# A second temporary for the spectrum products, one tile for what lay in two, and joint instructions in an S4/GEGLU kernel

## The chip, the cores and the metric

The kernel runs on one core of a Trainium2 chip. The metric is the device time of one execution in microseconds (us). The engines are PE (TensorE), PEld (its weight loads), DVE (VectorE), ACT (ScalarE), POOL (GpSimd) and SP (SyncE, which here issues nearly all DMA transfers).

## The reference

The kernel mixes two branches over the same input of 2048 positions and 640 channels. Branch a is an S4 convolution: a kernel K of length 2048 is built for each channel from 128 complex modes, and u is convolved with it, in the reference by FFT. Branch b is a GEGLU feed-forward layer with 1728 hidden columns.

```python
x = A_u
g = sigmoid((x * gate_w).sum(-1, keepdims=True))
P = exp((dt * A)[:, :, None] * l[None, None, :])
K = einsum("dn,dnl,dn->dl", Cc, P, dt * Bc).real
...
y = irfft(rfft(u, 2 * L) * rfft(K, 2 * L))[:L] + u * Dskip
b = (gelu(x @ w_gate) * (x @ w_up)) @ w_down
out = g * y + (1 - g) * b
```

## The kernel before

**Tiling.** Positions are handled in two halves of 1024 (th 0 and 1) for the feed-forward layer, channels in two halves of 320 (h 0 and 1, W2 = 320) for the convolution. The hidden columns are 14 blocks of 128, the last half full.

**Stages.** Gate and up projections: steps `g{ft}.{th}` and `u{ft}.{th}`, each 10 matmuls of 128x512 (`gu`, L381); `h.{th}` is block 13, whose 64 gate and 64 up columns share one result. The weights come in pairs of blocks, step `lw{n}`, into two slots (L277, L278). Results leave PSUM by `eg`/`eu` steps, copies on ACT (L386) or DVE (L388). What doesn't stay in SBUF goes to DRAM: the copy writes one of three slots named `ring`, an `sg`/`su` step sends the slot off (L408), and `rg`/`rl` steps bring it back later (L694 for the up part), where `hm` multiplies (L695). A ring slot is given to each use in turn when the steps are defined, so in the order of definition, not of emission.

Fold of the input: `uf{c}.{r}` (L372) writes sums and differences into `pm0`, `us{c}` sends them to DRAM, `lu{h}{c}` brings them back.

The table of K: for each h, exponentials (`xa`, `xb`), then chunks of phases and sines. A chunk of kind b takes `fb` (`phase_b`, L481, one DVE instruction for each of up to three blocks), `qb` (L469, the cosine's phase), `sb` (`sin_b`, L490: two sines of 128x960) and the products `pb`, `pc` (L495, L508); kind a takes `fa` (L474), `qa`, `sa` (L484, one sine of 128x1920), `pa` (L499). The sines write the buffer T. Then `ct{h}.{j}` contracts the tables on PE (L520, L521), `ek{h}.{j}` unloads (two copies of 128x504, one for each bank), `ks` adds the skip term (L587), `kd.{h}` sends the raw table Kraw to DRAM in four transfers that each read every fourth partition (`regroup_out`, L536), and `kt.{h}` brings it back in another arrangement.

Spectra: `U...` (L706) and `K...` (L719) on PE, evicted by ACT. Products on DVE: `m{h}{c}{i}{part}` multiplies a spectrum of u with one of K. The first two of a chunk write P and X directly (L761); the later ones write the one temporary t (L764), and `s{h}{c}{i}{part}` adds t to P or X (L765). `y{h}{c}0/1` (L767, L768) closes the chunk. Then the inverse `I` (L779), the down projection `D` (L794), the mix `Z` (L801, L802), the scaled eviction `o` and the store `st`.

**What sets the order.** The string ORDER lists all steps by name, and `manual_schedule` emits them in exactly that order; each engine and SP's queue of transfers work off theirs in the order of emission. A suffix `/A` or `/D` picks ACT or DVE, `/0` to `/3` a PSUM bank. The waits between engines are derived from which earlier instructions read or wrote the same tile.

**Memory.** `early` (29,696 bytes in each partition), `work` and `tail` (19,200) are tiles in which many buffers are laid over each other (`lay`). In `early` lie the fold's buffers (uf, ur and pm0, bytes 0 to 10239), later Kraw0 from byte 16128, later spectra. In `tail` lie T, al, th and other inputs of the table, later Kraw1 and IM, later Ub0, Kb0 and pmb.

Of the kernel before, what the change touches and what calls it, by code (L numbers as in the profile page):

```python
# [40 lines left out]
lp0 lpk ldt idx one tdt/0 tabE dt oa.0 sk leu2 lp5 lw0 lp3 t0/1 al xb23.0 xa4.0 xb6.0 xa10.0 al2 xa5.0 xa17.0 lp4 x0.0  # L41
lp2 t4/2 t2/3 xb4.0 xa19.0 c2 xb9.0 xb14.0 x1.0 t5/0 x4.0 x3.0 lp1 t3/1 c3 x2.0 v0 v3 ur0 ob.0 xa9.0 xb17.0 xb2.0
xb1.0 xb13.0 xa1.0 xa3.0 v1 v5 v2 t1/3 ul0 th v4 xb12.0 v6 v7 xb5.0 xa8.0 xb8.0 fb0.0 fb1.0 qb0.0 g1.0/1 eg1.0/D v8
uf0.1 v11 uf0.0 u1.0/2 xb21.0 xb11.0 v9 xa16.0 xb15.0 v10 xa11.0 xb3.0 xb27.0 xa14.0 eu1.0/D g0.0/0 u0.0/3 eu0.0/A v12
v13 v14 mag xb31.0 v15 xa7.0 xb7.0 xb29.0 xb25.0 xb19.0 xb10.0 xa15.0 v16 tabT sb0.0 x4.1 lw1 qb1.0 eg0.0/D g3.0/1
eg3.0/D ma3.0 ma0.0 v17 ma1.0 ul1 us0 ma4.0 ma6.0 u3.0/2 u2.0/3 g2.0/0 lw2 su0.0 leu3 lw3 su1.0 eu3.0/A eg2.0/A sb1.0
u4.0/1 eu2.0/A ur1 uf1.0 v18 uf1.1 ur2 fb2.0 pc0.0 qb2.0 pb0.0 pb1.0 pc1.0 fb3.0 qb3.0 us1 su2.0 sb2.0 eu4.0/A su4.0
lgw su3.0 lsk pb2.0 pc2.0 at g4.0/2 eg4.0/A sb3.0 ph45 fb4.0 qb4.0 g5.0/0 u7.0/3 eg5.0/A u5.0/1 eu5.0/A fb5.0 pc3.0
qb5.0 pb3.0 sb4.0 lw4 sb5.0 u6.0/2 eu6.0/A g7.0/0 g6.0/1 eu7.0/A eg7.0/A ma2.0 fa0.0 pc4.0 qa0.0 pb4.0 eg6.0/A sa0.0
g8.0/2 eg8.0/A u8.0/3 g9.0/0 x0.1 x2.1 lw5 x3.1 ul2 su7.0 su6.0 x1.1 lw6 su5.0 fa1.0 pb5.0 qa1.0 fa2.0 qa2.0 pa0.0  # L50
sa1.0 eg9.0/A fa3.0 sa2.0 pa1.0 u10.0/1 eu10.0/A qa3.0 sa3.0 pa2.0 u9.0/2 eu9.0/A fa4.0 qa4.0 pa3.0 fa5.0 sa4.0 fa6.0
qa5.0 pa4.0 qa6.0 eu8.0/A g11.0/0 u12.0/1 u11.0/2 eg11.0/A sa5.0 ma5.0 fil.0 pa5.0 g10.0/3 su8.0 su9.0 lu00 lw7 leu0
h.0/0 sa6.0 pa6.0 eu12.0/A eg10.0/D ct0.4/1 ek0.4/D eu11.0/A ct0.0/2 ct0.6/3 ek0.6/D uf2.0 uf2.1 ct0.3/1 ek0.0/A
eg13.0/A ct0.2/2 ct0.1/3 ek0.1/D ek0.3/A su10.0 su12.0 su11.0 ct0.5/1 ek0.2/D ek0.5/D ur3 oa.1 ob.1 u12.1/3 tabE2
xb8.1 fil.1 eu12.1/D ks.0 xa7.1 xb29.1 xb27.1 xb9.1 xa1.1 xb13.1 ma0.1 xa8.1 xb3.1 xa9.1 xa10.1 xb4.1 xa14.1 xb19.1
# [10 lines left out]
K000/3 eK001/D pa5.1 eK000/A K011 K012 K013 K010 pa6.1 eK012/A eK013/A eK010/D eK011/D tabG m0000 ct1.4/1 ct1.2/2
ek1.2/D ek1.4/A ge1.0 sg7.1 lw13 ct1.3/3 ek1.3/A ct1.1/0 ct1.5/1 ek1.5/A ct1.6/2 ek1.1/D rl1.0 su7.1 gl2 hm0.0 ct1.0/0
lu01 rl3.0 rl2.0 hm1.0 rl4.0 rg2.1 lkb1 rg13.1 lkb0 g9.1/3 ek1.0/A ek1.6/A dg9 m0001 gl3 y001 y000 U012/1 U011/0
eU011/D U010/2 eU012/D U013/3 ge3.0 eU010/A eU013/A ks.1 m0100 g11.1/0 ge5.0 ge9.0 dg11 kd.1 u11.1/1 g8.1/2 m0111
hm2.0 m0110 hm4.0 s0100 rl5.0 hm5.0 du11 hm3.0 dg8 m0101 g10.1/3 u8.1/0 gf/2 gf1 du8 s0101 dg10 ge7.0 ge11.0 u10.1/1  # L70
# [10 lines left out]
K110 K102/1 eK110/A K113 D020/2 eK102/A eK121/A eK113/A pm2/A s0320 m0321 s0321 m0330 s0330 m0331 s0331 y030 y031
m1001 m1000 K133/0 K112 eK112/A Z020 K122/3 eK122/A y101 m1100 eK133/A o020/A pm3/A D021/1 Z021 st010 st011 lwd1 lu12
lu13 st020 o021/A U132/3 U123/0 eU123/A I031/2 I030/1 m1110 y100 m1111 s1100 m1101 K130/0 eI031/A eK130/A eU132/A
eI030/A D030/2 U120/0 U122/3 eU120/A eU122/A I100/1 Z030 eI100/A U121/0 I101/3 D031/1 Z031 o030/A m1210 lwe1 eI101/A
eU121/A U131/2 eU131/A U130/3 eU130/A o031/A D100/0 K123/2 K120/3 eK120/A Z100 eK123/A s1101 y110 y111 m1220 m1211
s1220 I110/1 eI110/A m1221 s1221 m1200 s1200 m1201 st021 st030 st031 K132/3 eK132/A I111/2 U133/1 eU133/A o100/A
eI111/A m1310 D101/3 K131/1 eK131/A s1201 m1320 y120 y121 s1320 m1311 m1321 s1321 m1330 s1330 m1331 s1331 m1300 s1300
m1301 s1301 y130 y131 Z101 D110/0 D111/2 Z111 st100 o101/A st101 o111/A Z110 I120/1 I121/3 eI121/A eI120/A D120/2
o110/A st110 st111 Z120 o120/A st120 D121/3 Z121 o121/D D130/1 I130/0 eI130/A I131/2 Z130 o1301/A o1300/A eI131/D
D131/3 Z131 o1310/D st121 st1300 st1301 st1310 o1311/D st1311  # L90
# [54 lines left out]
def kernel(  # L145
# [253 lines left out]
    turn_no = [0]  # L399

    def ring():
        turn_no[0] += 1
        return at["ring"][:, turn_no[0] % at["ring"].shape[1]]

    def spill(which, name, eng_step, src, dst, rows):
        r = ring()
        step(eng_step, lambda eng="A", r=r: copy(eng, halves(r[0:rows]), PS[bank[name]][src]))
        step(f"s{which}", lambda r=r: S.dma_start(out=dst, in_=r[0:rows]))  # L408
# [469 lines left out]
```

## Time and profile before

| | us |
|---|---|
| runs | 288.59, 290.98, 292.38 |
| median of the three | 290.98 |
| span of the profiled execution | 287.8 |
| ACT busy | 221.0 (77%) |
| POOL busy | 16.0 (6%) |
| gate and up matmuls, L381, x526 | 120.9 |
| sums of products, L765, x24 | 35.7 |
| down matmuls, L794, two groups x224 | 31.7 and 31.4 |

The time that the profiled execution itself took is not listed apart from these runs; the page gives its span alone. In the rows below, `out<-in` names the tiles, `x` the number of instructions, and a bracket the idle time of the engine before them with what ended it. Rows of several instructions give the stretch from the first start to the last end. SPq is SP's queue of transfers; its times are those of issuing, not of landing. The windows view lists the busy time of PE, PEld, DVE, ACT and POOL, the granted TensorE clock as a share, the DMA share and GB/s.

### The profile page before, as it was taken

To read this page: it belongs to the slowest core of one execution; us is meant where nothing else is said; L and a number is where in the kernel's file an instruction comes from. 1 tells how busy PE (TensorE), PEld (TensorE's weight loads), DVE (VectorE), ACT (ScalarE), POOL (GpSimd) and SP (SyncE) were. 2 spreads that over 40 slices of the span, in tenths; PEclk is the share of its full clock that TensorE was granted. 3 is DMA by queue.
4 is the path that set the end of the run, shared out by engine and by line. 5 is a ranking of instruction groups with operands and counts; after the bars stand their busy time and mean duration, and the time that the engine had idled before them with its cause. 6 is when DMAs were issued, how large, how long until landed. Compare 5 with 4: busy or idle time off the path is not lost.

```text
span 287.8 us, 4927 instructions
## 1 busy us (share of the span) xinstructions
PE 264.4 (92%) x1869; PEld 159.4 (55%) x1883; DVE 261.7 (91%) x339; ACT 221.0 (77%) x321; POOL 16.0 (6%) x23
## 2 busy tenths in 40 slices
...
GB/s 207 207 224 193 132 298 178 211 236 118 182 224 202 200 308 227 226 272 259 234 76 223 206 193 294 235 80 179 109 284 73 2 23 23 25 23 2 68 23 46
DMA packets 64300, 46.94 MB, mean 163 GB/s; under 512 B 23403, under 2 KB 54166, under 8 KB 64278
## 3 DMA queue, kind: packets, MB, share of 16 engines
...
q0 software_dynamic: 384, 1.31, 1.7%
q10 hardware_dynamic: 576, 0.43, 0.5%
...
## 4 chain that ended last, share of the span: by engine, by line
DVE 47%; PE 30%; DMA 7%; issue 6%; ACT 4%; SPq 4%; POOL 0%; DVEq 0%; ACTq 0%
PE ps L381 25%; DVE work L764 11%; DVE work L765 11%; DVE work L761 8%; DMA work<-Ud 2%; DVE H L695 2%; SPq L285 2%; DVE work L388 2%; DVE work L767 2%; DMA xT<-in_A_u_dram 2%; DMA early<-in_A_u_dram,back 2%; DVE work L695 2%; DVE work L768 2%; ACT tail L490 1%; PE ps L794 1%
## 5 line engine op out<-in xcount | busy, mean ns | idle before, releaser
L381 PE MATMUL ps<-xT,Wr 128*128 128x512 bf16 x526 | 120.9, 386 | 6.5 <-ACT work L386 2.3
L381 PEld LDWEIGHTS <-Wr 128*128 128x128 bf16 x540 | 53.4, 99 | 70.9 <-issue 8.8
L386 ACT CAST work<-ps 128x640 bf16<-128x640 f32 (+1 forms) x59 | 47.8, 839 | 24.8 <-PE ps L779 15.7
L765 DVE TENSOR_TENSOR work<-work 128x2560 bf16<-128x2560 bf16 x24 | 35.7, 1487 | 0.5
L794 PE MATMUL ps<-xT,work 128*128 128x320 bf16 x224 | 31.7, 299 | 0.0
L794 PE MATMUL ps<-xT,H 128*128 128x320 bf16 x224 | 31.4, 299 | 0.0
L794 PEld LDWEIGHTS <-H 128*128 128x128 bf16 x224 | 21.9, 98 | 8.5
L794 PEld LDWEIGHTS <-work 128*128 128x128 bf16 x224 | 21.9, 98 | 8.5
L484 ACT ACTIVATE tail<-work 128x1920 bf16<-128x1920 int16 x14 | 25.2, 1816 | 0.5 <-DVE work L469 0.4
L508 DVE TENSOR_TENSOR work<-tail,work 128x1920 bf16<-128x1920 bf16 (+1 forms) x22 | 23.8, 1093 | 0.5 <-ACT tail L490 0.5
L392 ACT ACTIVATE Wr<-ps,gs 128x320 bf16<-128x320 f32 x28 | 13.2, 526 | 13.1 <-issue 9.5
L779 PE MATMUL ps<-work,tail 128*128 128x320 bf16 x128 | 19.7, 299 | 3.0 <-DVE work L767 3.0
L490 ACT ACTIVATE tail<-work 128x960 bf16<-128x960 int16 (+1 forms) x24 | 20.7, 927 | 0.0
L474 DVE SCALAR_TENSOR_TENSOR work<-tail 128x320 int32<-128x320 f32 x42 | 17.9, 483 | 0.5 <-ACT tail L484 0.5
L779 PEld LDWEIGHTS <-tail 128*128 128x128 bf16 x128 | 12.3, 98 | 9.0 <-DVE work L767 4.0
L706 PEld LDWEIGHTS <-early 128*128 128x128 bf16 x128 | 12.4, 98 | 7.0 <-issue 1.4
L469 DVE TENSOR_SCALAR work<-work 128x960 int32<-128x960 int16 (+1 forms) x26 | 16.1, 627 | 0.1
L499 DVE TENSOR_TENSOR work<-tail,work 128x1920 bf16<-128x1920 bf16 x14 | 15.9, 1150 | 0.0
L719 PE MATMUL ps<-KTt,early 128*128 128x320 bf16 x80 | 15.5, 313 | 0.5 <-ACT early L392 0.3
L365 POOL DMA_INDIRECT early<-in_A_u_dram,back x8 | 11.0, 1371 | 67.3 <-DVE early L372 57.0
L392 ACT ACTIVATE work<-ps 128x640 bf16<-128x640 f32 x15 | 10.4, 714 | 5.3 <-PE ps L719 5.2
L462 ACT ACTIVATE work<-tail 128x320 bf16<-128x320 f32 x30 | 12.5, 456 | 2.0 <-DVE tail L324 2.0
(120 smaller groups left out, 411.8 us busy)
## 6 DMA issues: line engine op xcount, KB each, us to landing
...
```

The source lines that it names most:

```text
L381: P.matmul(t[:, x, :], lhsT=Wr[:, slot, kt, cols:cols + 128], rhs=xT[:, th, kt, 512 * x:512 * x + 512], start=(kt == 0), stop=(kt == 4))
L386: A.copy(out=out, in_=in_)
L392: act(out=out, in_=in_, func=ACT.Copy, scale=scale)
L474: stt(out=t[:, 0, x], in0=at["th"][:, d], scalar=float(A_OF[3 * c + x] + MID), in1=at["ph45"][:, d], op0=ALU.mult, op1=ALU.add)
L484: act(out=T, in_=low16(t)[:, :, :, ::2], func=ACT.Sin, scale=SIN_SCALE)
L490: act(out=o[:, r], in_=i[:, r], func=ACT.Sin, scale=SIN_SCALE)
L508: tt(out=B2[:, :, :, cols].rearrange("p r g x -> p g r x"), in0=Tv if hf == 0 else Tv[:, :, ::-1], in1=e, op=ALU.mult)
L761: step(f"m{h}{c}{i}{part}", lambda dst=dst, ux=ux, kx=kx: tt(out=fl(dst), in0=ux, in1=kx, op=ALU.mult))
L764: step(f"m{h}{c}{i}{part}", lambda ux=ux, kx=kx: tt(out=fl(t), in0=ux, in1=kx, op=ALU.mult))
L765: step(f"s{h}{c}{i}{part}", lambda dst=dst, op=op: tt(out=fl(dst), in0=fl(dst), in1=fl(t), op=op))
L779: P.matmul(t[:, r, 0:W2], lhsT=IM[:, e, m, r], rhs=Y[:, r, m], start=(m == 0), stop=(m == 3))
L794: P.matmul(t[:, x, 0:W2], lhsT=H[c // 2][:, ft, tk:tk + 128], rhs=at[f"Wd{h}"][:, ft], start=(ft == 0), stop=False)
```

## The change

1. **Second temporary.** The products of part 1 write t1 instead of t, and ORDER moves the second product of a pair ahead of the first sum (m, m, s, s where it was m, s, m, s).
2. **One tile.** `early` and `tail` become one tile `side` of 49,664 bytes, in which t1 has room. T lies at byte 30464, Kraw0 stays at 16128, Kraw1 moves to 36224.
3. **Raw table of K.** Its layout goes from [4, NA, NG] to [NA, 4, NG], so that `ek` copies both banks with one instruction.
4. **One sine.** `sin_b` is one instruction of 128x1920; for it `phase_b` writes its result in blocks of four int32.
5. **Half tile.** `h.{th}` is copied once with 128 rows. For th 0 the up half is sent to DRAM from H0; for th 1 both halves from one ring slot, and `sg13.1` moves forward in SP's queue to stand directly ahead of `su13.1`.
6. **Ring slots** are taken from a list of free ones at emission and given back with the last use.
7. **Permutations.** flip and flipn are scaled by one instruction: four instead of six for each chunk.

SP's queue around `kd.0`, before: the spill of `u12.1`, the weights `lw8`, `kd.0`, then `sg12.1`, `su13.0`, `sg0.1` and `lw9`. The bracket names the semaphores waited for: DMAHW for a transfer, DVE, PE or Activation for a count on that engine.

```order
L278 DMA Wr<-in_B_w_up_dram 128x5x256 [waits DMAHW3_49]
L536 DMA Kd_70<-early 672x1x80 [waits DMAHW0_49,DMAHW4_49,DVE_49,Activation_49]
L536 DMA Kd_70<-early 672x1x80 [waits DMAHW5_49]
L536 DMA Kd_70<-early 672x1x80 [waits DMAHW6_49]
L536 DMA Kd_70<-early 672x1x80 [waits DMAHW7_49]
L408 DMA Gd<-work 128x1024 [waits DVE_49]
L408 DMA Ud_67<-work 64x1024 [waits DMAHW1_49]
L408 DMA Gd<-work 128x1024 [waits DMAHW2_49,DVE_49]
L277 DMA Wr<-in_B_w_gate_dram 128x5x256 [waits DMAHW3_49,PE_49]
L278 DMA Wr<-in_B_w_up_dram 128x5x256 [waits DMAHW4_49]
```

The same place of SP's queue after the change:

```order
L275 DMA Wr<-in_B_w_up_dram 128x5x256 [waits DMAHW3_49]
L538 DMA Kd_70<-side 672x1x80 [waits DMAHW4_49,DMAHW0_49,Activation_49]
L538 DMA Kd_70<-side 672x1x80 [waits DMAHW5_49]
L538 DMA Kd_70<-side 672x1x80 [waits DMAHW6_49]
L538 DMA Kd_70<-side 672x1x80 [waits DMAHW7_49]
L411 DMA Gd<-work 128x1024 [waits DVE_49]
L425 DMA Ud_67<-H_78 64x1024 [waits DMAHW1_49]
L411 DMA Gd<-work 128x1024 [waits DMAHW2_49,DVE_49]
L274 DMA Wr<-in_B_w_gate_dram 128x5x256 [waits DMAHW3_49,PE_49]
L275 DMA Wr<-in_B_w_up_dram 128x5x256 [waits DMAHW4_49]
```

The transfers stand in the same sequence; what moved is what the first of `kd.0` waits for. Before, its counts belong to `uf3.1` on DVE and `ek0.3` on ACT; now there is one count on ACT, and it is that of `sb0.1`, the first sine of half 1.

ACT behind the last exponential of half 1, before: the table load, the two sines of `sb0.1`, the eviction `eg1.1`, the two sines of `sb1.1`.

```order
L561 ACT_TABLE_LOAD
L490 ACTIVATE tail<-work 128x3x80x4 [waits DVE_49,Activation_49]
L490 ACTIVATE tail<-work 128x3x80x4 [waits DVE_49]
L386 CAST work<-ps_65 128x1024 [waits DMAHW5_49,DMAHW0_49,DMAHW6_49,DVE_49,PE_49]
L490 ACTIVATE tail<-work 128x3x80x4 [waits Activation_49]
```

And after:

```order
L563 ACT_TABLE_LOAD
L493 ACTIVATE side<-work 128x1920 [waits DVE_49,Activation_49]
L383 CAST work<-ps_65 128x1024 [waits DMAHW0_49,DMAHW5_49,DVE_49,PE_49]
L493 ACTIVATE side<-work 128x1920 [waits DMAHW5_49,DMAHW6_49,DMAHW4_49,DMAHW7_49,DVE_49,Activation_49]
L383 CAST work<-ps_66 128x1024 [waits DMAHW5_49,DMAHW1_49,DMAHW6_49,DVE_49,PE_49]
```

Each pair of sines is one, the sines write `side`, and the second chunk's sine (`sb1.1`) waits for the four transfers of `kd.0`, which read that tile.

DVE at the end of the products of chunk 3 of half 1, before: products (L764), sums (L765), then `y130` and `y131`.

```order
L764 TENSOR_TENSOR work<-work,tail 128x2560 [waits DVE_49]
L765 TENSOR_TENSOR work<-work 128x2560 [waits DVE_49]
L764 TENSOR_TENSOR work<-tail,early 128x2560 [waits DVE_49,Activation_49]
L765 TENSOR_TENSOR work<-work 128x2560 [waits DVE_49]
L764 TENSOR_TENSOR work<-tail,early 128x2560 [waits DVE_49]
L765 TENSOR_TENSOR work<-work 128x2560 [waits DVE_49]
L767 TENSOR_TENSOR work<-work 128x1280 [waits DVE_49]
```

And after:

```order
L766 TENSOR_TENSOR side<-work,side 128x2560 [waits DVE_49]
L767 TENSOR_TENSOR work<-work 128x2560 [waits DVE_49]
L767 TENSOR_TENSOR work<-work,side 128x2560 [waits DVE_49]
L766 TENSOR_TENSOR work<-side 128x2560 [waits DVE_49,Activation_49]
L766 TENSOR_TENSOR side<-side 128x2560 [waits DVE_49]
L767 TENSOR_TENSOR work<-work 128x2560 [waits DVE_49]
L767 TENSOR_TENSOR work<-work,side 128x2560 [waits DVE_49]
L769 TENSOR_TENSOR work<-work 128x1280 [waits DVE_49]
```

Two products stand together, then two sums, and every second product writes into `side`.

The diff, cut to its core (of ORDER a line at `kd.0` and one of the products):

```diff
-tabT2 sb0.1 ma2.1 h.1/3 su12.1 lw8 g0.1/0 eg0.1/D ma4.1 ma5.1 qb1.1 kd.0 sg12.1 su13.0 sg0.1 lw9 eu13.1/D ma6.1 su13.1
+sb0.1 ma2.1 h.1/3 su12.1 lw8 g0.1/0 eg0.1/D ma4.1 ma5.1 qb1.1 kd.0 sg12.1 su13.0 sg0.1 lw9 e13.1/D sg13.1 su13.1 ma6.1 u1.1/1
...
-eK113/A pm2/A s0320 m0321 s0321 m0330 s0330 m0331 s0331 y030 y031
+eK113/A pm2/A m0321 s0320 s0321 m0330 m0331 s0330 s0331 y030 y031 m1001 m1000 K133/0 K112 eK112/A Z020 K122/3 eK122/A y101
...
-    early = sb.tile([128, 29696 // 2], BF16, name="early")
+    side = sb.tile([128, 49664 // 2], BF16, name="side")
-    tail = sb.tile([128, 19200 // 2], BF16, name="tail")
...
-    lay(E0, 16128, ("Kraw0", BF16, 4, NA, NG))
+    lay(E0, 16128, ("Kraw0", BF16, NA, 4, NG))
...
-    lay(T0, 0, ("T", BF16, 2, 2, 3, W2), ("al", FP32, 2, D), ("th", FP32, D), ("ph45", FP32, D), ("mag", BF16, D))
-    lay(T0, 0, ("Kraw1", BF16, 4, NA, NG), ("IM", BF16, 2048))
-    lay(T0, 0, *[(x, BF16, 2, 4, W2) for x in ("Ub0", "Kb0")], ("pmb", BF16, 2, 2, W2))
+    lay(E0, 27648, ("t1", BF16, 2, 4, W2))
+    TA = 30464
+    lay(E0, TA, ("T", BF16, 2, 2, 3, W2), ("al", FP32, 2, D), ("th", FP32, D), ("ph45", FP32, D), ("mag", BF16, D))
+    lay(E0, 49664 - 13440, ("Kraw1", BF16, NA, 4, NG))
+    lay(E0, 32768, *[(x, BF16, 2, 4, W2) for x in ("Ub0", "Kb0")], ("pmb", BF16, 2, 2, W2), ("IM", BF16, 2048))
...
+    def ring(key, uses):
+        if key not in held:
+            held[key], left[key] = free.pop(0), uses
+        slot = held[key]
+        left[key] -= 1
+        if not left[key]:
+            free.append(slot)
+        return at["ring"][:, slot]
...
+                        step("e13.0", lambda eng="A", j=j: copy(eng, halves(H[0][:, 13]), PS[bank[j]][:]))
+                        step("su13.0", lambda: S.dma_start(out=Ud[0][0:64, 13], in_=H[0][64:128, 13]))
...
+                        step("e13.1", lambda eng="A", j=j: copy(eng, halves(ring("13.1", 3)), PS[bank[j]][:]))
+                        step("sg13.1", lambda: S.dma_start(out=Gd[0:64, 13], in_=ring("13.1", 3)[0:64]))
+                        step("su13.1", lambda: S.dma_start(out=Ud[1][0:64, 13], in_=ring("13.1", 3)[64:128]))
...
-            ts(out=t[:, 0, x], in0=at["th"][:, d], scalar1=8.0 * (3 * c + 1 + x), scalar2=TURN / 8, op0=ALU.mult, op1=ALU.add)
+            o = t[:, 0, 0:n].rearrange("p x d -> p (x d)").rearrange("p (g x w) -> p x g w", x=n, w=4)[:, x]
+            ts(out=o, in0=at["th"][:, d].rearrange("p (g w) -> p g w", w=4), scalar1=8.0 * (3 * c + 1 + x), scalar2=TURN / 8,
+               op0=ALU.mult, op1=ALU.add)
...
-        for r in range(2):
-            act(out=o[:, r], in_=i[:, r], func=ACT.Sin, scale=SIN_SCALE)
+        act(out=T[:, :, 0:n], in_=low16(t[:, :, 0:n])[:, :, :, ::2], func=ACT.Sin, scale=SIN_SCALE)
...
-            for b in range(nb):
-                copy(eng, dst[:, b], src[:, b])
+            copy(eng, dst, src)
...
-            S.dma_start(out=Kd[h][:, :, w, :], in_=K[w::4, w])
+            S.dma_start(out=Kd[h][:, :, w, :], in_=K[w::4, :, w])
...
+            scaled(eng, at["perm"][:, 0, c, k], ident, gs[:, 3, x + 2:x + 3])
+            scaled(eng, at["perm"][:, 1:3, c, k], picks[:, 128:384].rearrange("p (i q) -> p i q", i=2), gs[:, 4, x:x + 1])
...
-            Pt, X, t = at["P"][:, c % 2], at["X"], at["t"]
+            Pt, X, tb = at["P"][:, c % 2], at["X"], (at["t"], at["t1"])
...
-                    dst = (Pt, X)[part]
+                    dst, t = (Pt, X)[part], tb[part]
```

More of the change, by code (lines that the diff above doesn't have):

```diff
@@ L40 @@
 ORDER = """
[L41 to L55, printed above, removed]
@@ L66 @@
[L66 to L70, printed above, removed]
@@ L81 @@
[L81 to L90, printed above, removed]
+lp0 lpk ldt idx one tdt/0 tabE dt oa.0 sk leu2 lp5 lw0 lp3 t0/1 al xb23.0 xa4.0 xb6.0 xa10.0 al2 xa5.0 xa17.0 lp4 x0.0 lp2
@@ new lines @@
+t4/2 t2/3 xb4.0 xa19.0 c2 xb9.0 xb14.0 x1.0 t5/0 x4.0 x3.0 lp1 t3/1 c3 x2.0 v0 v3 ur0 ob.0 xa9.0 xb17.0 xb2.0 xb1.0 xb13.0
+xa1.0 xa3.0 v1 v5 v2 t1/3 ul0 th v4 xb12.0 v6 v7 xb5.0 xa8.0 xb8.0 fb0.0 fb1.0 qb0.0 g1.0/1 eg1.0/D v8 uf0.1 v11 uf0.0 u1.0/2
+xb21.0 xb11.0 v9 xa16.0 xb15.0 v10 xa11.0 xb3.0 xb27.0 xa14.0 eu1.0/D g0.0/0 u0.0/3 eu0.0/A v12 v13 v14 mag xb31.0 v15 xa7.0
+xb7.0 xb29.0 xb25.0 xb19.0 xb10.0 xa15.0 v16 tabT sb0.0 x4.1 lw1 qb1.0 eg0.0/D g3.0/1 eg3.0/D ma3.0 ma0.0 v17 ma1.0 ul1 us0
@@ new lines @@
+eu9.0/A fa4.0 qa4.0 pa3.0 fa5.0 sa4.0 fa6.0 qa5.0 pa4.0 qa6.0 eu8.0/A g11.0/0 u12.0/1 u11.0/2 eg11.0/A sa5.0 ma5.0 fil.0
+pa5.0 g10.0/3 su8.0 su9.0 lu00 lw7 leu0 h.0/0 sa6.0 pa6.0 eu12.0/A eg10.0/D ct0.4/1 ek0.4/D eu11.0/A ct0.0/2 ct0.6/3 ek0.6/D
+uf2.0 uf2.1 ct0.3/1 ek0.0/A ct0.2/2 ct0.1/3 ek0.1/D ek0.3/A su10.0 su12.0 su11.0 ct0.5/1 ek0.2/D ek0.5/D ur3 oa.1 ob.1
+u12.1/3 tabE2 xb8.1 fil.1 eu12.1/D ks.0 xa7.1 xb29.1 xb27.1 xb9.1 xa1.1 xb13.1 ma0.1 xa8.1 xb3.1 xa9.1 xa10.1 xb4.1 xa14.1
+xb19.1 xb2.1 xb17.1 us2 ul3 uf3.0 e13.0/D uf3.1 g12.0/2 fb0.1 xa19.1 xa3.1 xa15.1 xb6.1 xb21.1 xa16.1 xb15.1 xa11.1 g12.1/1
@@ new lines @@
+ct1.6/2 ek1.1/D rl1.0 su7.1 gl2 hm0.0 ct1.0/0 lu01 rl3.0 rl2.0 hm1.0 rl4.0 rg2.1 lkb1 rg13.1 lkb0 g9.1/3 ek1.0/A ek1.6/A dg9
+m0001 gl3 y001 y000 U012/1 U011/0 eU011/D U010/2 eU012/D U013/3 ge3.0 eU010/A eU013/A ks.1 m0100 g11.1/0 ge5.0 ge9.0 dg11
+kd.1 u11.1/1 g8.1/2 m0111 hm2.0 m0110 hm4.0 m0101 s0100 rl5.0 hm5.0 du11 hm3.0 dg8 g10.1/3 u8.1/0 gf/2 gf1 du8 s0101 dg10
+ge7.0 ge11.0 u10.1/1 rl7.0 rg5.1 ge12.0 ge13.0 rl8.0 lim0 lu02 leu1 lu03 rl6.0 er0 u9.1/3 K030/2 eK030/A er1 lwz0 lwe0 hm7.0
+du10 hm6.0 hm8.0 U020/0 eU020/A U022/1 eU022/A rg1.1 lim1 rl10.0 U023/2 eU023/A rg4.1 K020/0 du9 y011 eK020/D y010 hz1 lwz1
@@ L91 @@
+eI120/A D120/2 o110/A st110 st111 Z120 o120/A st120 D121/3 Z121 o121/D D130/1 I130/0 eI130/A I131/2 Z130 o1301/A o1300/A
+eI131/D D131/3 Z131 o1310/D st121 st1300 st1301 st1310 o1311/D st1311
 """
@@ L226 @@
     ident, flip, flipn = (picks[:, 128 * x:128 * x + 128] for x in range(3))
-    E0 = early[:]
+    E0 = side[:]
     lay(E0, 0, ("prm", BF16, 6, D), ("crs", BF16, 2, D), ("dtb", BF16, D))
     lay(E0, 0, ("uf", BF16, 2, D), ("ur", BF16, 2, D), ("pm0", BF16, 2, 2, D))
-    lay(E0, 16128, ("Kraw0", BF16, 4, NA, NG))
+    lay(E0, 16128, ("Kraw0", BF16, NA, 4, NG))
     lay(E0, 0, ("FM", BF16, 2048), ("KMa", BF16, 4096), *[(x, BF16, 2, 4, W2) for x in ("Uf0", "Kf0", "Kf1")])
```

88 lines of the change are left out of this document (43 added, 45 removed).

## The prediction

> **What bounds the kernel now.** I read the page first, then the timelines of the engines around the places that the diff touches, then the waits.
>
> The page's head, its line for the busy engines and its chain of work:
>
> ```profile
> span 287.8 us, 4927 instructions
> PE 264.4 (92%) x1869; PEld 159.4 (55%) x1883; DVE 261.7 (91%) x339; ACT 221.0 (77%) x321; POOL 16.0 (6%) x23
> DVE 47%; PE 30%; DMA 7%; issue 6%; ACT 4%; SPq 4%; POOL 0%; DVEq 0%; ACTq 0%
> ```
>
> PE and DVE are both nearly full, so 23 us of PE idleness (287.8 - 264.4) is all there is to win on PE, and any new hole in PE that DVE cannot shorten later lengthens the run. The instructions that the edit touches most stand on DVE, but the place that decides is a queue. SP's timeline around `kd.0` (start, duration, line, what goes where), and the row of the waits for it:
>
> ```profile
> 85.42 0.61 SPq L278 DMA_DIRECT2D Wr<-in_B_w_up_dram  x1
> 88.38 2.67 SPq L536 DMA_DIRECT2D Kd<-early  x4
> 91.10 0.63 SPq L408 DMA_DIRECT2D Gd<-work  x1
> 91.77 0.50 SPq L408 DMA_DIRECT2D Ud<-work  x1
> 94.40 0.35 SPq L408 DMA_DIRECT2D Gd<-work  x1
> 94.84 0.39 SPq L277 DMA_DIRECT2D Wr<-in_B_w_gate_dram  x1
> 95.29 0.60 SPq L278 DMA_DIRECT2D Wr<-in_B_w_up_dram  x1
> SPq L536 <- DVE early L372: 2.2, 1, 2.2
> ```
>
> DVE's timeline, the two rows that released SP there:
>
> ```profile
> 87.49 0.81 DVE L372 TENSOR_TENSOR early<-early 128x1280 bf16<-128x1280 bf16 x1
> 93.16 1.22 DVE L388 CAST work<-ps 128x1024 bf16<-128x1024 f32 x1
> ```
>
> PE's timeline there, with the idle time before each row in brackets:
>
> ```profile
> 80.08 17.43 PE L381 MATMUL ps<-xT,Wr 128*128 128x512 bf16 x78 [0.46 <-DVE early L388]
> 99.39 8.81 PE L381 MATMUL ps<-xT,Wr 128*128 128x512 bf16 x39 [1.89 <-DMA Wr<-in_B_w_up_dram]
> ```
>
> `kd.0` is issued at 88.38, as `uf3.1` ends (87.49 + 0.81 = 88.30), though `uf3.1` writes bytes 7680 to 10239 of `early` and `kd.0` reads the table from byte 16128 on. So a transfer that reads every fourth partition waits for the last earlier writer of anything in its tile; the whole tile is what counts. Behind it in the same queue stand `sg12.1`, `su13.0`, `sg0.1` and `lw9`, the weights of `u2.1`; PE has been out of work since 97.51 when they land and it resumes at 99.39.
>
> **The change: the queue at `kd.0`.** After the edit the sine tables T lie in `side`, with the raw table that `kd.0` reads. ORDER puts `sb0.1`, the first sine of half 1, ahead of `kd.0`; it was in `tail` and is now an earlier writer of `kd.0`'s tile. The order of the changed program has `kd.0` wait on Activation and no longer on DVE. ACT's timeline says when that sine can be done:
>
> ```profile
> 98.64 1.28 ACT L561 ACT_TABLE_LOAD   x1
> 99.94 1.90 ACT L490 ACTIVATE tail<-work 128x960 bf16<-128x960 int16 x2
> 101.74 0.99 ACT L386 CAST work<-ps 128x1024 bf16<-128x1024 f32 x1
> 104.43 1.00 ACT L386 CAST work<-ps 128x1024 bf16<-128x1024 f32 x1
> 105.86 1.01 ACT L386 CAST work<-ps 128x1024 bf16<-128x1024 f32 x1 [0.43 <-issue]
> 124.09 1.01 ACT L386 CAST work<-ps 128x1024 bf16<-128x1024 f32 x1 [0.31 <-DMA Ud<-work]
> ```
>
> and the group of sines that already are one instruction of 128x1920:
>
> ```profile
> L484 ACT ACTIVATE tail<-work 128x1920 bf16<-128x1920 int16 x14 | 25.2, 1816 | 0.5 <-DVE work L469 0.4
> ```
>
> The sine starts at 99.94, straight behind a table load and exponentials that wait for nothing in SP's queue, and takes 1.82: it ends at 101.8, against 88.3 for what released `kd.0` before. From `kd.0`'s issue to `u2.1` the trace has 99.39 - 88.38 = 11.0 us. Of these SP spent 94.40 - 92.27 = 2.1 waiting for the copy at 93.16 on DVE, which will long be done; 8.9 remain, for the issue of nine transfers and the landing of the weights. So `u2.1` starts at 101.8 + 8.9 = 110.7, 11.3 later, and PE stands still from 97.5, for 13.2 us instead of 1.9. I keep the landing as it was: the same transfers are ahead of it.
>
> What is late next: PE's clock, and ACT behind PE.
>
> ```profile
> 109.62 2.32 PE L381 MATMUL ps<-xT,Wr 128*128 128x512 bf16 x10 [0.88 <-ACT work L386]
> 113.10 4.70 PE L381 MATMUL ps<-xT,Wr 128*128 128x512 bf16 x19 [0.61 <-ACT work L386]
> 127.76 2.14 PE L625 MATMUL ps<-gwc,xT 128*128 128x1 bf16 x80
> 131.88 0.59 PE L381 MATMUL ps<-xT,Wr 128*128 128x512 bf16 x1 [0.80 <-ACT work L386]
> 131.00:137.00 6.00, 4.98 (x14) 2.02 (x14) 5.53 (x9) 4.94 (x5) 0.00 (x0) 0.50 1.01 309
> ```
>
> The last row is a window: busy time of PE, PEld, DVE, ACT and POOL, then the granted clock, 0.50. That dip follows some four microseconds of one-column matmuls and waits (127.76 to 131.88). A hole of 13 us should bring it too; six microseconds at half speed cost PE 3.0, none cost 0. The eviction of `g3.1` on ACT (104.43) needs 20 matmuls of the row at 99.39, 8.81 / 39 = 0.226 each: 4.5 at full clock, up to 7.5 at half. So it moves to 115.2 to 118.2, later by 10.8 to 13.8; I take the middle, **+12.3**, since nothing tells how long the dip lasts.
>
> From there to 132 ACT leads (PE waits for it 0.88, 0.61 and 0.80). One 1.82 in place of two sines in 1.90 saves 0.08 on each of four chunks, 0.3; slots that are handed out when they are free remove the 0.43 and 0.31 that ACT waited for a slot's spill. Together **-1.1**; the bounds are 0 and the 2.3 that PE waits.
>
> **The second temporary.** DVE's timeline of products and sums:
>
> ```profile
> 212.50 1.49 DVE L764 TENSOR_TENSOR work<-work,early 128x2560 bf16<-128x2560 bf16 x1
> 214.03 1.49 DVE L765 TENSOR_TENSOR work<-work 128x2560 bf16<-128x2560 bf16 x1
> ...
> 250.35 1.49 DVE L764 TENSOR_TENSOR work<-tail,work 128x2560 bf16<-128x2560 bf16 x1
> 251.76 1.48 DVE L761 TENSOR_TENSOR work<-early,work 128x2560 bf16<-128x2560 bf16 x1
> 253.16 1.48 DVE L765 TENSOR_TENSOR work<-work 128x2560 bf16<-128x2560 bf16 x1
> 254.68 1.49 DVE L764 TENSOR_TENSOR work<-work 128x2560 bf16<-128x2560 bf16 x1
> ```
>
> PE's rows that wait for them:
>
> ```profile
> 222.54 2.52 PE L779 MATMUL ps<-work,tail 128*128 128x320 bf16 x16 [1.88 <-DVE work L767]
> 276.63 2.52 PE L779 MATMUL ps<-work,tail 128*128 128x320 bf16 x16 [0.69 <-DVE work L767]
> ```
>
> A sum right behind its own product starts 1.53 after it (212.50 to 214.03), and a product that overwrites the temporary which the sum just read 1.52 after that (253.16 to 254.68). Where another product stands between, as at 251.76, the starts are 1.40 apart. Counted in the two orders, 34 such adjacent pairs become 9; before `y030` 13 become 3, after it 21 become 6. At 0.12 that is 1.2 us of DVE by `y030` and 3.0 in all. PE is full between the two waits, so it gains at the first min(1.2, 1.88) = 1.2 and at the second at most 0.69: **-1.9**; the bounds are 0 and 1.88 + 0.69 = 2.6. The Trainium skill, page "VectorE: DVE Perf Modes", section "The DRAIN you can't avoid", says that operations chained without semaphores still pay the flush between them; by that the second temporary would save nothing and the sum would be 1.9 higher. The trace here differs: 1.40 against 1.53.
>
> The same edit makes `m0101` write into `side`, so it waits for `kd.1`'s four transfers, which read that tile.
>
> ```profile
> 154.11 2.65 SPq L536 DMA_DIRECT2D Kd<-tail  x4
> 159.53 1.48 DVE L765 TENSOR_TENSOR work<-work 128x2560 bf16<-128x2560 bf16 x1
> ```
>
> `m0101` now takes the place of the sum at 159.53. The issue ends at 156.76; with the 3.5 us that the large weight transfer took to land (95.89 to 99.39) the wait would be 0.7, with less than 2.8 none. These are much smaller transfers: 0, bounds 0 and 0.7.
>
> **The rest.** The first half of each phase is now written in blocks of four int32:
>
> ```profile
> L481 DVE TENSOR_SCALAR work<-tail 128x320 int32<-128x320 f32 x32 | 8.4, 319 | 0.0
> L512 DVE TENSOR_SCALAR work<-work 128x320 bf16<-128x320 bf16 x4 | 1.0, 256 | 0.1
> L474 DVE SCALAR_TENSOR_TENSOR work<-tail 128x320 int32<-128x320 f32 x42 | 17.9, 483 | 0.5 <-ACT tail L484 0.5
> ```
>
> L512 writes blocks of four already (256 ns for as many elements), so I keep 319: 0. If the layout cost as much as L474's 483, it would be 0.164 x 16 = 2.6 us in each half. The joint half tile takes away two copies of about 1 us that did not hold anyone up; fewer unload copies and permutation scalings shorten ACT and DVE where PE is full. Cover gone, they would be worth up to 0.5 in all. I take 0, bounds -0.5 and +2.6.
>
> **The sum.** 12.3 - 1.1 - 1.9 = +9.3 us on a span of 287.8: 297.1. The time of that execution is not listed apart; its span is 0.8 below the fastest run shown (288.59) and 3.2 below the median. On the median, 290.98 + 9.3 = 300.3 us.
>
> **Rivals.**
> - No new wait at `kd.0` (the transfer is released by its own data, or the hole is filled): only the savings are left, -3.0, so 288.0, about 1% and no measurable change. For it: they do read other bytes. Against it: the 2.2 us that SP waited for L372, which writes other bytes too.
> - Faster: it decides at the same place. If `kd.0` is let go at 88.4 or sooner, ACT gains its whole 2.3 and PE then waits too little around 130 for the clock to fall; the 3.0 lost in the window at 0.50 come back as well: 2.3 + 1.9 + 3.0 = 7.2, so 283.8. It needs `kd.0` early and the dip gone.
> - The hole comes, but PE resumes at full clock (+10.8), and every saving reaches its bound (-2.3, -2.6, -0.5): +5.4, 296.4, just at the line to slower.
> - The hole comes with the full dip (+13.8), the savings stay at -3.0 and the strided phase costs 2.6 in half 1: +13.4, 304.4.
>
> **Numbers.** About 2%, 5.8 us here, is what a measurement of this kernel can tell from no change: faster means under 285.2, slower over 296.8. The hole at `kd.0` has 0.86: 0.62 for the forecast (297 to 303), 0.13 for the mild and 0.11 for the bad form. No wait has 0.11, the faster case 0.03. The mild form falls to half under the line and the forecast's lower tail adds a little: slower 0.77, same 0.20, faster 0.03. The range reaches from below the mild form's end to the bad one, 294 to 304.5, and leaves out the cases without the hole.
>
> **What would show it.** Right: in SP's timeline `kd.0` (now L538) issued at about 101.8, straight after the first L493 of half 1, with a wait of about 15 us on ACT; PE idle for about 13 us before `u2.1` at 110 to 111, released by the weights; a granted clock of 0.50 behind it; sums (L767) that start 1.40 after the row before; idle before L781 at `y030` under 1 us. Wrong: `kd.0` issued near 88; or the idle of PE at `u2.1` short, because the weights come earlier than the queue says; or L486 near 480 ns.

## The result, and the profile after

The change made the kernel slower by 3.5%.

| kernel | median, us | runs | ratio to the kernel before (95% interval) |
|---|---|---|---|
| before | 290.54 | 4 (288.59 to 292.38) | |
| changed | 300.94 | 4 (299.18 to 302.22) | 1.0347 (1.0287 to 1.0407) |

The kernel before has one run more here than in the table ahead of the prediction, 290.10 us. Each ratio in this document is to runs of the kernel before that were taken beside the kernel in question; differences in us between two kernels are differences of their medians.

The profiled execution of the changed kernel took 302.22 us, with a span of 300.4; it is the longest of the four. The page's head, busy engines and chain of the changed kernel:

```profile
span 300.4 us, 4891 instructions
PE 264.6 (88%) x1869; PEld 159.9 (53%) x1883; DVE 257.5 (86%) x332; ACT 217.7 (72%) x294; POOL 16.9 (6%) x23
PE 49%; DVE 22%; ACT 12%; DMA 8%; SPq 5%; issue 3%; DVEq 0%; ACTq 0%
```

There is less work on DVE (257.5 against 261.7) and on ACT (217.7 against 221.0) and the same on PE, and yet the span is 12.6 us longer. The time went into one place. SP's timeline of the changed kernel around `kd.0`, and the row of its waits:

```profile
86.84 0.59 SPq L275 DMA_DIRECT2D Wr<-in_B_w_up_dram  x1
102.75 2.67 SPq L538 DMA_DIRECT2D Kd<-side  x4
105.47 0.65 SPq L411 DMA_DIRECT2D Gd<-work  x1
106.16 0.50 SPq L425 DMA_DIRECT2D Ud<-H  x1
106.76 0.53 SPq L411 DMA_DIRECT2D Gd<-work  x1
107.38 0.40 SPq L274 DMA_DIRECT2D Wr<-in_B_w_gate_dram  x1
107.84 0.60 SPq L275 DMA_DIRECT2D Wr<-in_B_w_up_dram  x1
SPq L538 <- ACT side L493: 15.2, 1, 15.2
```

The queue stands for 15.2 us, where it stood 2.2, and it is ACT's sine that lets it go. ACT's timeline, from the table load to the eviction of `g3.1`:

```profile
99.63 1.28 ACT L563 ACT_TABLE_LOAD   x1
100.93 1.80 ACT L493 ACTIVATE side<-work 128x1920 bf16<-128x1920 int16 x1
108.09 1.01 ACT L383 CAST work<-ps 128x1024 bf16<-128x1024 f32 x1 [5.36 <-DMA Gd<-work]
109.00 1.81 ACT L493 ACTIVATE side<-work 128x1920 bf16<-128x1920 int16 x1
119.40 1.93 ACT L383 CAST work<-ps 128x1024 bf16<-128x1024 f32 x2 [8.59 <-PE ps L378]
```

PE's timeline there, and two windows (busy PE, PEld, DVE, ACT, POOL, then the granted clock, the DMA share and GB/s):

```profile
81.55 17.43 PE L378 MATMUL ps<-xT,Wr 128*128 128x512 bf16 x78 [0.40 <-DVE side L385]
113.22 10.46 PE L378 MATMUL ps<-xT,Wr 128*128 128x512 bf16 x39 [14.25 <-DMA Wr<-in_B_w_up_dram]
...
110.00:116.00 6.00, 2.78 (x7) 1.03 (x8) 6.00 (x13) 0.81 (x1) 0.00 (x0) 0.50 1.00 316
116.00:122.00 6.00, 5.95 (x26) 2.60 (x26) 2.70 (x3) 2.60 (x3) 0.00 (x0) 0.95 0.65 241
```

The sine ends at 102.73 and `kd.0` goes out at 102.75. PE waits 14.25 us for the weights that stand behind it, then starts at a granted clock of 0.50; the 39 matmuls that took 8.81 take 10.46. The eviction of `g3.1`, the first of the two at 119.40, comes 15.0 later than before (104.43), of which 1.5 were there ahead of the hole (81.55 against 80.08). DVE stood too: its copy `eu1.1` waited 10.59 us for the spill `sg0.1`, that is for a ring slot.

```profile
109.52 1.23 DVE L385 CAST work<-ps 128x1024 bf16<-128x1024 f32 x1 [10.59 <-DMA Gd<-work]
```

### The profile page after: what moved, and what is told of

It reads as the page before. It is cut to its first block, busy times and chain, and to the rows that moved or that the text cites. A ratio compares the mean times of both kernels' runs of the same rounds, so it can differ in the third digit from the quotient of the medians.

```text
span 300.4 us, 4891 instructions
## 1 busy us (share of the span) xinstructions
PE 264.6 (88%) x1869; PEld 159.9 (53%) x1883; DVE 257.5 (86%) x332; ACT 217.7 (72%) x294; POOL 16.9 (6%) x23
## 3 DMA queue, kind: packets, MB, share of 16 engines
q0 software_dynamic: 384, 1.31, 1.8%
## 4 chain that ended last, share of the span: by engine, by line
PE 49%; DVE 22%; ACT 12%; DMA 8%; SPq 5%; issue 3%; DVEq 0%; ACTq 0%
PE ps L378 28%; PE ps L796 11%; DVE work L767 4%; DVE work L763 4%; PE ps L781 3%; DMA work<-Ud 3%; DVE side L766 3%; DVE work L766 2%; DVE H L697 2%; DMA xT<-in_A_u_dram 2%; SPq L282 2%; DMA Wr<-in_B_w_up_dram 2%; ACT work L466 2%; DVE work L697 2%; ACT work L470 2%
## 5 line engine op out<-in xcount | busy, mean ns | idle before, releaser
L511 DVE TENSOR_TENSOR work<-side,work 128x1920 bf16<-128x1920 bf16 (+1 forms) x22 | 23.8, 1091 | 4.5 <-ACT side L493 4.4
L490 ACT ACTIVATE side<-work 128x1920 bf16<-128x1920 int16 x14 | 25.2, 1814 | 0.5 <-DVE work L473 0.4
L781 PE MATMUL ps<-work,side 128*128 128x320 bf16 x128 | 19.5, 299 | 1.6 <-DVE work L769 1.6
L385 DVE CAST work<-ps 128x1024 bf16<-128x1024 f32 (+1 forms) x9 | 9.7, 1084 | 12.6 <-DMA Gd<-work 10.6
L493 ACT ACTIVATE side<-work 128x1920 bf16<-128x1920 int16 (+1 forms) x12 | 19.7, 1642 | 0.1
L478 DVE SCALAR_TENSOR_TENSOR work<-side 128x320 int32<-128x320 f32 x42 | 17.9, 482 | 0.1
L767 DVE TENSOR_TENSOR work<-work,side 128x2560 bf16<-128x2560 bf16 x12 | 17.8, 1484 | 0.1
L767 DVE TENSOR_TENSOR work<-work 128x2560 bf16<-128x2560 bf16 x12 | 17.8, 1482 | 0.0
L708 PEld LDWEIGHTS <-side 128*128 128x128 bf16 x128 | 12.4, 98 | 8.0 <-issue 1.8
L781 PEld LDWEIGHTS <-side 128*128 128x128 bf16 x128 | 12.4, 98 | 7.2 <-DVE work L769 2.3
L502 DVE TENSOR_TENSOR work<-side,work 128x1920 bf16<-128x1920 bf16 x14 | 16.0, 1150 | 0.1
L721 PE MATMUL ps<-KTt,side 128*128 128x320 bf16 x80 | 14.9, 299 | 1.3 <-ACT side L389 0.8
```

Source lines behind the costliest of these rows:

```text
L478: stt(out=t[:, 0, x], in0=at["th"][:, d], scalar=float(A_OF[3 * c + x] + MID), in1=at["ph45"][:, d], op0=ALU.mult, op1=ALU.add)
L490: act(out=T, in_=low16(t)[:, :, :, ::2], func=ACT.Sin, scale=SIN_SCALE)
L493: act(out=T[:, :, 0:n], in_=low16(t[:, :, 0:n])[:, :, :, ::2], func=ACT.Sin, scale=SIN_SCALE)
L502: tt(out=PQ[:, :, 3 * c:3 * c + 3].rearrange("p r x d -> p x r d"), in0=T.rearrange("p r x d -> p x r d"), in1=e[:, :, None, :].to_broadca ...
L511: tt(out=B2[:, :, :, cols].rearrange("p r g x -> p g r x"), in0=Tv if hf == 0 else Tv[:, :, ::-1], in1=e, op=ALU.mult)
L767: step(f"s{h}{c}{i}{part}", lambda t=t, dst=dst, op=op: tt(out=fl(dst), in0=fl(dst), in1=fl(t), op=op))
```

## The experiments

**The sine behind the transfer.** One word of ORDER moves in the changed kernel. The sequence of instructions on every engine stays as it is.

```diff
-sb0.1 ma2.1 h.1/3 su12.1 lw8 g0.1/0 eg0.1/D ma4.1 ma5.1 qb1.1 kd.0 sg12.1 su13.0 sg0.1 lw9 ...
+ma2.1 h.1/3 su12.1 lw8 g0.1/0 eg0.1/D ma4.1 ma5.1 qb1.1 kd.0 sb0.1 sg12.1 su13.0 sg0.1 lw9 ...
```

> The changed kernel with one word of ORDER moved: sb0.1, the first sine of half 1, is emitted right behind kd.0 instead of ahead of it. Each engine's sequence of instructions stays the same; only the waits differ. Theory (the wait of kd.0 on that sine makes the loss): SP waits at kd.0 about 2 us and not 15, the hole of 14.2 us ahead of u2.1 falls back to about 1.9, and the time to 300.9 - 12.4 = 288.5 us, 1% under the kernel before. Rival (the hole comes from the ring slots, from sg13.1's new place in the queue, or the loss is spread over the other edits): the time stays at 298 or more.

Measured: 287.95 us, ratio to the kernel before 0.992 (0.9873 to 0.9967). Its wait at `kd.0`, SP's row of `kd.0`, and PE's row at `u2.1`:

```profile
SPq L538 <- DVE side L369: 2.5, 1, 2.5
88.27 2.67 SPq L538 DMA_DIRECT2D Kd<-side  x4
99.08 8.81 PE L378 MATMUL ps<-xT,Wr 128*128 128x512 bf16 x39 [1.60 <-DMA Wr<-in_B_w_up_dram]
```

SP waits for the fold's sum (L369) again, as the kernel before did, the hole is 1.60 us and the matmuls run at full clock. Without the wait on the sine the same edits gain 2.6 us. The difference of the two kernels, 300.94 - 287.95 = 13.0 us, is the price of that one wait by the medians; the runs of either scatter by 3 to 4 us.

**The same wait in the kernel before.** An ACT copy is added behind the sines of `sb0.1`; it writes 128x1920 dead bytes of the tile `early`, none of them `kd.0`'s. In one kernel it is emitted ahead of `kd.0`, in its twin behind it; ACT's sequence is the same in both.

```diff
+    step("mark", lambda: A.copy(out=early[:, 0:1920], in_=work[:, 0:1920]))
...
-tabT2 sb0.1 ma2.1 h.1/3 ... qb1.1 kd.0 sg12.1 ...
+tabT2 sb0.1 mark ma2.1 h.1/3 ... qb1.1 kd.0 sg12.1 ...
...
+tabT2 sb0.1 ma2.1 h.1/3 ... qb1.1 kd.0 mark sg12.1 ...
```

> The kernel before with one ACT copy of 128x1920 added behind the two sines of sb0.1 and emitted ahead of kd.0; it writes bytes 0 to 3839 of the tile that kd.0 reads, dead bytes that nothing reads before they are written anew, and none of kd.0's own. Theory: kd.0 waits for that copy, which ends near 103.6, the hole ahead of u2.1 grows by 13 to 14 us, and with the clock's dip and the copy's own 1.8 us the time is 302 to 306 us. Rival (the hole needs the other edits): equal to its twin in which the copy is emitted behind kd.0.

> The twin: the kernel before with the same added ACT copy at the same place of ACT's sequence, but emitted behind kd.0, so that kd.0 does not wait for it. Theory: no hole, 290.5 plus 0 to 1.8 us for the copy in a stretch in which ACT leads: 290.5 to 292.5 us. Rival (the copy itself is what costs): as slow as the other one.

Measured: 302.90 us (1.0461, 1.0395 to 1.0528) with the copy ahead, 294.38 us (1.0172, 1.0105 to 1.024) with it behind. The wait and PE's row with the copy ahead:

```profile
SPq L536 <- ACT early L614: 13.5, 1, 13.5
111.22 11.46 PE L381 MATMUL ps<-xT,Wr 128*128 128x512 bf16 x39 [13.88 <-DMA Wr<-in_B_w_up_dram]
```

And in the twin:

```profile
SPq L603 <- ACT early L614: 4.2, 1, 4.2
99.95 6.65 PE L381 MATMUL ps<-xT,Wr 128*128 128x512 bf16 x29 [1.75 <-DMA Wr<-in_B_w_up_dram]
113.50 2.32 PE L381 MATMUL ps<-xT,Wr 128*128 128x512 bf16 x10 [1.99 <-ACT work L386]
```

A single write of other bytes in `kd.0`'s tile, with nothing else of the change, makes a hole of 13.88 us. The twin has none at `u2.1`. It was expected at up to 292.5 and is 3.9 us slower than the kernel before: the copy takes about 1.8 us of ACT where ACT leads, and the first transfer that loads FM (L603) writes the same dead bytes and now waits 4.2 us for the copy, with the queue behind it. So the twin is not clean, and the difference of the two, 8.5 us, is less than the price of the wait; the hole itself is shown by the rows.

**Only the weights ahead.** In the changed kernel `lw9` moves ahead of `kd.0`, which still waits for the sine.

```diff
-... qb1.1 kd.0 sg12.1 su13.0 sg0.1 lw9 e13.1/D ...
+... qb1.1 lw9 kd.0 sg12.1 su13.0 sg0.1 e13.1/D ...
```

> The changed kernel with lw9, the weights of u2.1, moved in SP's queue from behind sg0.1 to right ahead of kd.0; kd.0 still waits for the sine. Theory A (the weights alone are what PE lacks): PE goes on at u2.1 without a hole and the time is about 289 us. Theory B (everything queued behind kd.0 counts): sg12.1 and sg0.1 still land only at 108 to 109.5, so the ring slots come free late, the copies eg1.1 and eu1.1 that empty PE's banks wait for them, and u2.1 starts near 110.8 and not 113.2: a gain of 2 to 3 us only, 298 to 299 us.

Measured: 296.86 us (1.0239, 1.0189 to 1.0289). SP's rows of the weights and of `kd.0`, and PE's at `u2.1`:

```profile
88.78 0.52 SPq L275 DMA_DIRECT2D Wr<-in_B_w_up_dram  x1
99.44 2.67 SPq L538 DMA_DIRECT2D Kd<-side  x4
107.34 11.07 PE L378 MATMUL ps<-xT,Wr 128*128 128x512 bf16 x39 [10.37 <-DVE work L385]
106.06 1.23 DVE L385 CAST work<-ps 128x1024 bf16<-128x1024 f32 x1 [9.05 <-DMA Gd<-work]
```

The weights are sent at 88 to 89, and PE still stands 10.37 us: now for the copy `eu1.1` on DVE (the last row), which waits for the ring slot that `sg0.1` holds. Theory B holds; the gain is 4.1 us rather than 2 to 3. The weights were the last of several things that stood behind `kd.0`.

**The second temporary taken back.** From here on the sine stands behind `kd.0`. The later products write t alone, and products and sums alternate as before.

```diff
-            Pt, X, tb = at["P"][:, c % 2], at["X"], (at["t"], at["t1"])
+            Pt, X, tb = at["P"][:, c % 2], at["X"], (at["t"], at["t"])
...
-eK113/A pm2/A m0321 s0320 s0321 m0330 m0331 s0330 s0331 y030 y031 ...
+eK113/A pm2/A s0320 m0321 s0321 m0330 s0330 m0331 s0331 y030 y031 ...
```

> The changed kernel with sb0.1 behind kd.0 and the second temporary taken back: all later products write t again, and products and sums stand in the order of the kernel before (product, sum, product, sum, m0101 behind dg8). All else of the change stays. Theory (a sum right behind its product starts 0.12 later than one with another product between): against the kernel with m0101 alone put back, DVE is 1.2 us later at y030 and 2.5 to 3 at y130, the waits of PE before I030 and I130 are again near 1.9 and 0.7, and the time is 1.4 to 2 us longer. Rival (chained operations pay the flush anyway): the same time and the same starts.

**m0101 put back** behind `dg8`, where the kernel before had it.

```diff
-... hm2.0 m0110 hm4.0 m0101 s0100 rl5.0 hm5.0 du11 hm3.0 dg8 g10.1/3 ...
+... hm2.0 m0110 hm4.0 s0100 rl5.0 hm5.0 du11 hm3.0 dg8 m0101 g10.1/3 ...
```

> The changed kernel with sb0.1 behind kd.0 and m0101 put back behind dg8, where the kernel before had it; nothing else. Theory (m0101 ahead of s0100 makes hm4.0 1.4 us later, with it the ring slot of rl5.0 and the four transfers behind it in SP's queue, so lwe0 on DVE waits 1.1 us for its edge and PE 1.0 for the evictions behind it): the wait of lwe0 is gone, PE's wait there falls from 0.97 to under 0.5, and the time is 0.5 to 1 us under the 287.95 us of the kernel with the sine alone moved: 287 to 287.5. Rival (DVE has other slack there): no change.

Measured: 289.57 us with one temporary (0.9977, 0.9937 to 1.0017) and 286.96 us with two and `m0101` back (0.9851, 0.9793 to 0.9908). DVE's last rows ahead of `y030` with one temporary, and PE's wait for it:

```profile
217.00 1.49 DVE L766 TENSOR_TENSOR work<-work,side 128x2560 bf16<-128x2560 bf16 x1
218.53 1.49 DVE L767 TENSOR_TENSOR work<-work 128x2560 bf16<-128x2560 bf16 x1
220.06 0.83 DVE L769 TENSOR_TENSOR work<-work 128x1280 bf16<-128x1280 bf16 x1
...
220.94 4.02 PE L781 MATMUL ps<-work,side 128*128 128x320 bf16 x16 [1.88 <-DVE work L769]
```

With two:

```profile
217.23 1.47 DVE L766 TENSOR_TENSOR side<-work,side 128x2560 bf16<-128x2560 bf16 x1
218.63 1.47 DVE L767 TENSOR_TENSOR work<-work 128x2560 bf16<-128x2560 bf16 x1
220.03 1.47 DVE L767 TENSOR_TENSOR work<-work,side 128x2560 bf16<-128x2560 bf16 x1
221.54 0.82 DVE L769 TENSOR_TENSOR work<-work 128x1280 bf16<-128x1280 bf16 x1
...
222.42 2.52 PE L781 MATMUL ps<-work,side 128*128 128x320 bf16 x16 [1.05 <-DVE work L769]
```

Starts are 1.53 apart with one temporary and 1.40 with two; PE's wait falls from 1.88 to 1.05, not to 0.7. The two intervals do not meet; the medians differ by 2.6 us, and the second temporary with its order is all that differs between the two kernels. That is above the expected 1.4 to 2, but runs that scatter by 3 us do not exclude 2.

The two spans (286.4 and 286.6) do not show it: the one profiled execution is the shortest of its twelve, the other the longest of its six. Counted from the matmuls behind the product of the edge (PE at 167.35 and 169.55; the latter row stands below), the rest of the span is 119.05 us with one temporary and 117.05 with two, 2.0 less. Counted from that product on DVE (165.13 and 167.33), `y030` starts 0.7 later with one temporary and `y130` (274.37 and 273.57) 3.0 later; expected were 1.2 and 2.5 to 3. The wait of 0.7 ahead of `I130` did not come back. Instead the 16 matmuls behind `y030` took 4.02 us with one temporary and 2.52 with two, because the clock fell there. The windows of those matmuls, with one temporary and in the kernel before:

```profile
221.00:225.00 4.00, 3.99 (x17) 2.25 (x18) 3.86 (x4) 0.69 (x1) 0.00 (x0) 0.60 0.00 0
```

```profile
222.60:226.60 4.00, 3.99 (x29) 2.76 (x30) 3.86 (x4) 1.93 (x4) 0.00 (x0) 1.00 0.00 0
```

The kernel before waits the same 1.88 us there and keeps its full clock, so this loss of 1.5 us belongs to the execution and is not a fixed price of the wait. It hardly changes the sum, for with it the wait ahead of `I130` (0.69 in the kernel before) is gone: from those matmuls to the end of the span the kernel before takes 65.26 us, the one with one temporary 65.46 and the one with two 64.18.

`m0101`'s place is a small loss inside the change. DVE and PE behind it, with their waits, in the kernel with the sine alone moved:

```profile
166.33 0.32 DVE L674 TENSOR_TENSOR xT<-edge_u,edge_k 14x320 bf16<-14x320 bf16 x1 [0.88 <-DMA edge_u<-in_A_u_dram]
168.55 1.25 PE L708 MATMUL ps<-side 128*128 128x320 bf16 x8 [0.97 <-DVE work L442]
```

And with `m0101` back:

```profile
167.33 0.32 DVE L674 TENSOR_TENSOR xT<-edge_u,edge_k 14x320 bf16<-14x320 bf16 x1
169.55 1.25 PE L708 MATMUL ps<-side 128*128 128x320 bf16 x8 [0.45 <-DVE work L442]
```

Ahead of `s0100`, `m0101` makes `s0100` and `hm5.0` one product, 1.4 us, later. `hm5.0` frees the ring slot of `rl8.0` (not `hm4.0` and `rl5.0`, as the expectation named them), and behind `rl8.0` in SP's queue stands the load of the edge. DVE waits 0.88 us for it, and PE 0.97. Put back, DVE does not wait there and PE waits 0.45. The medians agree with the expected gain (286.96 against 287.95), but their intervals overlap, so only the wait is shown, not its price.

**The weights and m0101.** Both orders put right, and `lw9` ahead of `kd.0`.

> As the one with m0101 back, and lw9 emitted ahead of kd.0 as well, with kd.0 not waiting for the sine. Theory: the weights of u2.1 are there before PE needs them, so the 1.6 us of idle PE ahead of u2.1 goes; ACT leads behind it (PE waits 1.4 for it at 109.8), so that only 0 to 1 us of it reaches the end: 286 to 287.5 us. Rival (kd.0 being 1 us later delays what is behind it as much): no change.

Measured: 285.70 us (0.9824, 0.977 to 0.9879), the fastest of all, faster than the kernel before and than the changed one, and 0.3 under the expected range. PE's row at `u2.1`:

```profile
98.61 8.79 PE L378 MATMUL ps<-xT,Wr 128*128 128x512 bf16 x39 [1.31 <-DVE work L385]
```

The wait there did not go as expected; it has another end. PE waits 1.31 us for DVE's `eu1.1` where it waited 1.60 for the weights. The medians fell by 1.3 us against the kernel with `m0101` back, with intervals that overlap: how much the weights' place is worth stays open.

## Why the prediction was right

**The hole at `kd.0`** is the forecast's first term, and its chain holds: the sine ends, `kd.0` follows, PE stands until the weights come, the clock is at 0.50 behind it. Forecast were 11.3 us more of hole and 12.3 at the eviction of `g3.1`; PE's wait grew by 14.25 - 1.89 = 12.4, the eviction came 15.0 - 1.5 = 13.5 later, and moving the sine alone gave back 13.0. The step that was too small is "I keep the landing as it was": from `kd.0`'s issue to `u2.1` it took 113.22 - 102.75 = 10.5 us instead of 8.9. The issue is nearly as forecast: the last transfer of the weights is out at 108.44, 5.7 after `kd.0`'s start, where 5.4 were left of 7.5 without the 2.1 of waiting. The landing is what grew most, from 3.5 to 4.8 us (108.44 to 113.22). The DMA engines are nearly full in both stretches, with a share of 0.92 at 242 GB/s before and of 0.97 at 288 after: in the longer one more was moved. So transfers that were issued with pauses between them before now leave the queue in one go and share the engines with the weights. That this is the cause was only read from these windows, not tried.

**The clock.** Up to 3.0 us were put on it, half of that in the sum. PE lost 10.46 - 8.81 = 1.65.

**The wording of the rule at `kd.0`** was too wide. It said that the last earlier writer of anything in the tile counts. The kernel before was also written with the added copy in other sizes, and the waits were listed but not run: there is none of `kd.0` for a copy of one, 1024 or 1280 elements of each partition, and there is one for 1920. So not every write of the tile holds the transfer; `sb0.1`'s does, as do the fold's sum and the added copy of 1920, and none of the three writes a byte that it reads. The number of elements alone does not decide it, for the fold's sum writes 1280. By which measure the waits are derived was not found. The 2.2 us at L372 were evidence that foreign bytes can count, and the forecast made more of them than they said.

**The savings.** Forecast were -3.0 us without the hole; the kernel with the sine moved has 287.95 - 290.54 = -2.6. The second temporary was put at -1.9. With `m0101` where the change puts it, it is worth 289.57 - 287.95 = 1.6; with `m0101` back, 2.6, and 2.0 in the two traces from a common point. The sizes agree; the way there is not quite the forecast one: PE's wait at `y030` fell by 0.8 and not by 1.2, and behind it the trace with one temporary lost time to the clock and not to the wait at `I130`. The rest, -1.1 for the sines and the ring, is not shown. The kernel with one temporary has 289.57 - 290.54 = -1.0 (0.7 by its ratio), but its interval includes no change. The ring's part rested on two waits of ACT, 0.43 and 0.31, read as waits for a slot's spill; the row of the first says "issue" and names no spill. With the sine moved neither is there, but ACT waits longer for the spill of another slot:

```profile
108.77 1.01 ACT L383 CAST work<-ps 128x1024 bf16<-128x1024 f32 x1 [1.53 <-DMA Gd<-work]
```

The rule of the Trainium skill, "VectorE: DVE Perf Modes", section "The DRAIN you can't avoid", read as saying that an operation pays the flush whether or not it depends on the one before, would make the second temporary worth nothing. The runs differ: 1.53 between starts with the dependence, 1.40 without.

**What was called hidden.** The phases written in blocks of four cost nothing, and the sine in one instruction is 1.82 as taken:

```profile
L486 DVE TENSOR_SCALAR work<-side 128x320 int32<-128x320 f32 x32 | 8.4, 318 | 0.0
L493 ACT ACTIVATE side<-work 128x1920 bf16<-128x1920 int16 x10 | 18.2, 1818 | 0.0
```

For `m0101` the forecast asked about the wrong wait: `kd.1`'s transfers do not hold it, but it holds up the queue behind `rl8.0`. That effect the forecast did not have.

**The sum.** Forecast were +9.3 us, measured +10.4 (300.94 - 290.54). The hole was put too small, at 12.3 against 13.0, and the savings too large, at 3.0 against 2.6. That 300.3 lies within 0.7 us of the measured time is in part luck: it was added to a median of three runs, 290.98, that the fourth run lowered by 0.4.

**The rivals.** No wait at `kd.0` is refuted by the row of 15.2 us. Its time, 288.0, is what the kernel with the sine moved shows (287.95), so it was priced rightly as a case that did not come; that the two agree so closely is luck, by the same 0.4. The clock's dip at 131 to 137 of the kernel before is missing at the same work of the changed one. The first row is the window of that work in the changed kernel, the second and third are PE's matmul behind the waits and the first contraction of half 1 there, the last is that contraction before:

```profile
145.00:150.00 5.00, 3.73 (x20) 2.04 (x21) 5.00 (x8) 5.00 (x5) 0.00 (x0) 1.00 0.95 269
...
145.89 2.32 PE L378 MATMUL ps<-xT,Wr 128*128 128x512 bf16 x9 [0.90 <-ACT work L383]
...
153.89 0.20 PE L523 MATMUL ps<-work 128*128 128x84 bf16 x1 [0.26 <-DVE work L502]
```

```profile
141.92 0.20 PE L520 MATMUL ps<-work 128*128 128x84 bf16 x1 [0.51 <-DVE work L499]
```

The matmul at 145.89 stood at 131.88, 14.0 earlier; the contraction is only 12.0 later. So 2 us of the hole came back here. The rival of a faster kernel counted on the dip's end without the hole. Without the hole it is seen both ways: with the sine moved the clock is 0.50 in 132 to 134, in the execution with `m0101` back it is 1.00 in 132 to 138. What decides the dip is not shown, so neither is that the hole took it away.
